# Two cached attention layers and two gated layers on one core: joint sums of a head's two batches, queries of two heads at once, and early key units of pass 2 in one eight-tile product

## The chip, the core and the metric

The kernel runs on one core of a Trainium2 chip. The core has a matrix engine (TensorE, PE in the profile, with PEld for its weight loads), a vector engine (DVE), a scalar engine (ScalarE, ACT), GpSimd (POOL) and SyncE (SP), which here only issues DMAs. Its 16 DMA engines move the data from HBM into the on-chip memory SBUF. The metric is the device time of one execution in microseconds (us). The kernel before has a median of 1315.13 us over three runs (1314.31 to 1316.29).

## What is computed

One token for each of two batches (B = 2, D = 448 features) goes through attention, a gated layer, attention and the gated layer again; both layers use the same weights and the same caches each time. The caches are what is large: 16 heads, 4096 cached positions, 256 features, keys and values, float32, read in full in each of the two attention passes.

```python
def _A_ref(x, k_cache, v_cache, wq, wo):          # x: (2, 1, 448), caches: (2, 16, 4096, 256)
    q = (x @ wq).reshape(B, Sq, H, Dh).transpose(0, 2, 1, 3)
    scores = jnp.einsum("bhqd,bhkd->bhqk", q, k_cache) * (Dh ** -0.5)
    p = _softmax(scores, axis=-1)
    o = jnp.einsum("bhqk,bhkd->bhqd", p, v_cache)
    return o.transpose(0, 2, 1, 3).reshape(B, Sq, H * Dh) @ wo

def _B_ref(x, W_gate, W_up, W_down):
    gate = x @ W_gate                              # (448, 1792)
    gate = gate * (gate > 0)
    return (gate * (x @ W_up)) @ W_down

x = x + _A_ref(_layernorm(x), ...)
x = x + _B_ref(_layernorm(x), ...)
x = x + _A_ref(_layernorm(x), ...)
x = x + _B_ref(_layernorm(x), ...)
```

## The kernel before, in words

**Units.** Attention works through 32 units in a pass, one for each head and batch; the two batches of a head stand next to each other, so units 0 and 1 are one head, units 2 and 3 the next. A unit has 4096 keys and 4096 values of 256 floats. On 128 partitions that is 32 tiles of 256 floats for the keys and as many for the values. Eight tiles make a chunk (2048 floats for each partition, 1.05 MB); a unit's keys are four chunks, numbered c = 0 to 3.

**One unit.** The query is spread over all partitions. DVE multiplies the key tiles by it and sums each product to one score; ACT does a share of the sums (`activation` with `accum_out`). In most of a pass (`score_block`) one product covers all 32 tiles (L468) and one reduction sums 24 or 32 of them (L482). In the first five units of pass 2 (`u < HASTE`) and at the end of it (`CLOSING`), `score` goes chunk by chunk: a product of several tiles (L514), sums of some of them on ACT (L520), and for the rest either a reduction (L524) or, tile by tile, a fused product and sum on DVE (L527). Then `softmax_max` takes the maximum (DVE L536, over the partitions by POOL L538), `softmax_exp` the exponentials (ACT L543, L546) and their sum over the partitions (POOL L552), of which DVE takes a reciprocal for a head's two units (L559). `weigh` multiplies the values by the weights on PE (L580): four pairs of tiles go to four groups of rows of one PSUM bank, two rows in each, and the two batches use two banks. `out_copy` (ACT L593) and `out_add` (DVE L596) add a bank's two halves, `out_turn` (PE L606) sums the rows and turns them into a column, `out_keep` (DVE L619) divides, and `project` (PE L629) multiplies by the head's output weights. A wait on another engine stands in an engine's own queue, in the order of the code: what follows it on that engine waits too.

**Queries.** `query(u + 1)`, in every odd unit, makes the queries of the next head for both batches: five matmuls on PE (L414, L418), a copy on ACT (L426) and two broadcasts on POOL (L430). In the chunked units the order on ACT is: sums of chunks 0 to 2, the copy of the query, sums of chunk 3.

**Memory and loads.** SBUF holds an arena of three blocks of eight slots (a slot is one chunk) and three smaller single slots. `pump` issues the loads of a fixed list, in order and all from SP (L154); the next is issued as soon as slots for it are free, so a load is set off by the release of what lay there before. In mid-pass a load is a whole block, 8.39 MB (four chunks of keys of a unit and four of values of the unit before). Some twenty chunks at the start of pass 2 are kept from pass 1 (`keep`), so pass 2 begins with data on chip, and its loads wait for these chunks to be used up. Its units run in the order of heads 15, 14, 0, 1, ... 13. A load has one of eight semaphores in turn, and an SP instruction also waits for the load that used the same semaphore before.

**The gated layer** (`ffn`) follows each pass. Its weights come in seven loads of 0.92 MB (`w_in`) and four smaller ones (`w_out`). During its matmuls the first units of pass 2 have no query yet.

**What the change touches.** `pump` and `source` (loads), `query_weights`, `query_of` and `query`, the choice of tiles in `score` (L502 to L510), `softmax_exp`, `weigh`, `out_copy` to `out_keep`, and the packing of the weights on the host.

Of the kernel before, what the change touches and what calls it, by code (L numbers as in the profile page):

```python
# [15 lines left out]
P = 128  # L16
# [19 lines left out]
SUMS = 96  # L36
HASTE = 5
# [41 lines left out]
def two_layers(  # L79
# [31 lines left out]
    left_at = {}  # L111

    def source(key, n):
# [16 lines left out]
        if kind == "in":  # L130
            return w_in[c]
        return w_out[:, 14 * P * c : min(14 * P * (c + 1), 14 * D)]

    def pump():
        while pending:
# [19 lines left out]
            for k in range(n):  # L155
# [5 lines left out]
                at_of[key] = at + k  # L161
            if n >= NC:
                blocks.add((kind, name))
# [5 lines left out]
    def get(*key):  # L169
        at = at_of[key]  # L170
        return arena[:, place(at) : place(at + 1)]

    def query_weights(h):
        if h >= GROUPED:
            return get("h", h, 0)[:, : F // 2]
        at = h % 2 * F // 2
        return get("q", h // 2, 0)[:, at : at + F // 2]
# [55 lines left out]
    at_end[("k", n_u - 2)] = twos  # L233
# [14 lines left out]
    pending += of_second + [(key, 1) for key in ffn_loads]  # L248
# [22 lines left out]
    junk = down[:, :DH]  # L271
    y_end_row = extra[SUMS : SUMS + B, :TAIL]
# [9 lines left out]
    lead = little("lead", 2, bufs=1)  # L282
    nc.vector.reduce_sum(lead, ident.rearrange("p (m r) -> p r m", r=32)[:, :2], axis=AX.X)
# [86 lines left out]
    def attention(order, after, q_first=None, begun=None):  # L370
# [10 lines left out]
        def query_of(u, pq):  # L381
            h, b = order[u]
            w = query_weights(h)
            for c in range(FULL):
                nc.tensor.matmul(
                    pq[:, b, :],
                    xT[:, c, b : b + 1].to_broadcast([P, P]),
                    w[:, c * DH : (c + 1) * DH],
                    start=(c == 0),
                    stop=False,  # L390
                )
            for j in range(2):
                nc.tensor.matmul(
                    pq[:, b, j * P : (j + 1) * P],
                    xT[:, FULL + j, b : b + 1].to_broadcast([P, P]),
                    w[:, FULL * DH : FULL * DH + P],
                    start=False,
                    stop=(j == 1),
# [3 lines left out]
        def query(u):  # L402
            h = order[u][0]
            w = query_weights(h)
# [7 lines left out]
            q = pq[:33, 0, :]  # L412
            for c in range(FULL):
                nc.tensor.matmul(  # L414
                    q, xs[:, c, :], w[:, c * DH : (c + 1) * DH], start=(c == 0), stop=False
                )
            for j in range(2):
                nc.tensor.matmul(  # L418
                    q[:, j * P : (j + 1) * P],
                    xs[:, FULL + j, :],  # L420
# [570 lines left out]
```

## Time and profile before

| | before |
|---|---|
| median of three runs | 1315.13 us |
| the profiled execution, its own time | 1315.95 us |
| its span (first to last instruction) | 1314.1 us |
| read from HBM | 560.73 MB, 427 GB/s over the span |
| busy: DVE, PE, POOL, ACT | 82%, 43%, 28%, 16% |
| granted TensorE clock, mean | 0.682 |
| instructions | 9066 |

The profiled execution lies 0.82 us above the median of the runs. In the views below, times are from the start of the span. "idle before" in square brackets is how long the engine stood idle before an instruction, and behind the arrow what ended that. PE does each float32 matmul in two passes, so a group of three matmuls is counted as x6. Pass 1 takes the time to about 662 us, the first gated layer to 688 us, pass 2 to about 1288 us. The units of pass 2 stand in the trace as follows: unit 0 from 688.2 us, unit 1 from 699.6, unit 2 from 710.2, unit 3 from 721.4, unit 4 from 734.7, unit 5 from 746.0, unit 6 from 764.7, unit 7 from 782.1, unit 8 from 800.8, unit 9 from 829.8 us (starts of their first product on DVE).

### The profile page before, as it was taken

What the parts mean: (1) busy time and instruction counts of PE and PEld (TensorE: products, weight loads), DVE (VectorE), ACT (ScalarE), POOL (GpSimd) and SP (SyncE); (2) the same over time, 40 slices, a digit from 0 to 9 for tenths busy, and PEclk for the clock granted to TensorE, in tenths of its full rate; (3) what the DMA queues carried; (4) which work ended last, traced back from release to release, by engine and by line L of the source; (5) the groups of instructions that cost most, each with busy time, mean ns of one, the idle gap of its engine ahead of it and who ended that gap; (6) DMA issues with size and microseconds to landing.
All of it is one profiled execution on the core that took longest, in us unless ns stands there. A gap on an engine that the chain in (4) does not pass through costs nothing.

```text
span 1314.1 us, 9066 instructions
## 1 busy us (share of the span) xinstructions
PE 569.9 (43%) x3280; PEld 192.3 (15%) x3280; DVE 1075.0 (82%) x744; ACT 213.3 (16%) x853; POOL 367.5 (28%) x192
## 2 busy tenths in 40 slices
PE   3143343433434334245495544342443434434358
PEld 2011111110111101112141111110111101111113
DVE  4989989799897998787729987698999889886981
ACT  2100000010000000122416523000000000022261
POOL 0332305325053250321001144142345324130220
PEclk9676666666666666677796666666766757667579
DMA  9999999999999999999999999999999999999997
GB/s 407 443 427 431 434 433 427 437 431 429 437 433 429 437 433 418 445 423 430 420 400 418 433 427 443 429 435 433 427 436 431 433 435 433 431 431 427 428 422 326
DMA packets 20216, 561.32 MB, mean 427 GB/s; under 512 B 2248, under 2 KB 2380, under 8 KB 6860
## 3 DMA queue, kind: packets, MB, share of 16 engines
q1 hardware_dynamic: 20164, 560.74, 99.4%
q8 instruction: 26, 0.43, 0.1%
q14 instruction: 18, 0.15, 0.0%
q10 hardware_dynamic: 8, 0.00, 0.0%
HBM read 560.73 MB, written 0.00 MB: 427 GB/s over the span
## 4 chain that ended last, share of the span: by engine, by line
DMA 60%; DVE 28%; PE 6%; POOL 4%; ACT 2%; issue 1%; SPq 0%; DVEq 0%; POOLq 0%; ACTq 0%
DMA arena<-in_vk_dram 54%; DVE tiny L482 11%; DVE arena L468 11%; POOL tiny L538 4%; DMA arena<-in_w_head_dram 3%; DMA arena<-in_w_in_dram 2%; DVE arena L514 2%; DVE arena L527 1%; PE po L580 1%; DMA arena<-in_w_out_dram 1%; DVE row L596 1%; ACT arena L520 1%; PE pq L414 1%; PE small L606 1%; PE acc L629 1%
## 5 line engine op out<-in xcount | busy, mean ns | idle before, releaser
L468 DVE TENSOR_TENSOR arena<-arena 128x8192 f32<-128x8192 f32 (+2 forms) x52 | 441.7, 8497 | 100.8 <-DMA arena<-in_vk_dram 100.7
L482 DVE TENSOR_REDUCE tiny<-arena 128x32 f32<-128x8192 f32 (+2 forms) x53 | 430.2, 8118 | 0.0
L606 PE MATMUL small<-tiny,row 128*128 128x1 f32 x256 | 61.6, 344 | 656.4 <-DVE row L596 656.4
L580 PE MATMUL po<-arena,tiny 128*2 128x512 f32 x2052 | 307.8, 748 | 40.4 <-ACT tiny L546 17.6
L552 POOL PARTITION_ALL_REDUCE tiny<-tiny x64 | 249.9, 3905 | 61.3 <-ACT tiny L546 61.3
L538 POOL PARTITION_ALL_REDUCE tiny<-tiny x64 | 89.3, 1396 | 551.9 <-DVE tiny L536 551.9
L606 PEld LDWEIGHTS small<-tiny,row 128*128 128x128 f32 x256 | 56.1, 306 | 717.6 <-DVE row L596 717.6
L543 ACT ACTIVATE tiny<-tiny 128x1 f32<-128x1 f32 x64 | 18.8, 294 | 580.2 <-POOL tiny L538 580.2
L430 POOL PARTITION_BROADCAST arena<-arena x58 | 27.6, 546 | 288.8 <-ACT arena L426 288.8
L580 PEld LDWEIGHTS po<-arena,tiny 128*2 128x2 f32 x2052 | 54.0, 97 | 239.8 <-issue 197.1
L414 PE MATMUL pq<-arena,xs 128*33 128x256 f32 x174 | 74.6, 595 | 0.0
L520 ACT ACTIVATE arena<-arena 128x256 f32<-128x256 f32 x154 | 62.0, 404 | 42.2 <-DVE arena L514 42.0
L426 ACT ACTIVATE arena<-pq 33x256 f32<-33x256 f32 x29 | 10.9, 377 | 307.6 <-PE pq L418 307.6
L596 DVE SCALAR_TENSOR_TENSOR row<-po,tiny,row 128x256 f32<-128x256 f32 x64 | 30.7, 479 | 35.2 <-ACT row L593 34.9
L629 PE MATMUL acc<-arena,tiny 128*2 128x448 f32 x128 | 49.5, 868 | 21.3 <-DVE tiny L619 18.6
L474 ACT ACTIVATE arena<-arena 128x256 f32<-128x256 f32 x104 | 41.7, 403 | 78.1 <-DVE arena L468 78.1
L514 DVE TENSOR_TENSOR arena<-arena 128x1024 f32<-128x1024 f32 (+2 forms) x25 | 41.9, 1674 | 4.3 <-PE acc L629 4.3
L414 PEld LDWEIGHTS pq<-arena,xs 128*33 128x33 f32 x174 | 25.1, 161 | 66.4 <-issue 65.2
L593 ACT ACTIVATE row<-po,tiny 128x256 f32<-128x256 f32 x64 | 29.1, 455 | 26.7 <-PE po L580 26.7
L520 ACT ACTIVATION_READ_ACCUMULATOR arena<-arena 128x1 f32 x154 | 28.8, 187 | 0.0
L619 DVE TENSOR_TENSOR tiny<-small,tiny 128x4 f32<-128x4 f32 x32 | 5.2, 161 | 28.6 <-PE small L606 28.6
L546 ACT ACTIVATE tiny<-tiny 128x32 f32<-128x32 f32 x64 | 26.4, 413 | 2.2
(153 smaller groups left out, 369.2 us busy)
## 6 DMA issues: line engine op xcount, KB each, us to landing
arena<-in_vk_dram SPq DMA_DIRECT2D x16, 4096.0 KB, 40.1
arena<-in_vk_dram SPq DMA_DIRECT2D x18, 2048.0 KB, 36.1
arena<-in_w_pair_dram SPq DMA_DIRECT2D x11, 1792.0 KB, 30.7
arena<-in_w_in_dram SPq DMA_DIRECT2D x14, 896.0 KB, 23.2
arena<-in_vk_dram SPq DMA_DIRECT2D x12, 1024.0 KB, 10.4
arena<-in_vk_dram SPq DMA_DIRECT2D x1, 6784.0 KB, 39.4
arena<-in_w_head_dram SPq DMA_DIRECT2D x7, 896.0 KB, 8.7
arena<-in_w_out_dram SPq DMA_DIRECT2D x5, 896.0 KB, 8.5
```

Source lines behind the costliest of these rows:

```text
L414: nc.tensor.matmul(q, xs[:, c, :], w[:, c * DH : (c + 1) * DH], start=(c == 0), stop=False)
L468: nc.vector.tensor_mul(part, part, q_of[u][:, None, :].to_broadcast([P, n, DH]))
L474: nc.scalar.activation(kt[:, t, :], kt[:, t, :], AF.Copy, accum_out=s_of[u][:, t : t + 1])
L482: nc.vector.reduce_sum(found, part, axis=AX.X)
L514: nc.vector.tensor_mul(part[:, :whole, :], kt[:, :whole, :], q_of[u][:, None, :].to_broadcast([P, whole, DH]),)
L520: nc.scalar.activation(part[:, t, :], part[:, t, :], AF.Copy, accum_out=found[:, t : t + 1])
L538: nc.gpsimd.partition_all_reduce(mx_of[u], mx, P, RED.max)
L552: nc.gpsimd.partition_all_reduce(total[:, b : b + 1], rs, P, RED.add)
L580: nc.tensor.matmul(po_of[u][32 * t : 32 * t + 2, (i - 2 * t) * DH : (j - 2 * t) * DH], p_of[u][:, n : n + 2], values[:, i * DH : j * DH], ...
L596: nc.vector.scalar_tensor_tensor(row[:, :DH], po_of.pop(u)[:, DH:], lead[:, 1:2], row[:, :DH], op0=ALU.mult, op1=ALU.add,)
L606: nc.tensor.matmul(pT_of[u - u % 2][:, c, b : b + 1], row[:, c * P : (c + 1) * P], ones, start=True, stop=True,)
L629: nc.tensor.matmul(acc[at : at + B], oT_of[h][:, c, :], wo[:, c * D : (c + 1) * D], start=(n < 3), stop=(n >= n_u - 3),)
```

## The change

**Joint sums.** The exponentials of a unit go to one of two rows of 66 floats (`spaced`), in which every pair of weights is followed by a pair of zeros; GpSimd clears the rows at the start of a pass. A matmul of `weigh` takes four columns of it: (w, w, 0, 0) for a head's first unit and (0, 0, w, w) for its second. So both units of a head add up in four rows of one bank, and `out_copy`, `out_add` and `out_turn` run once for a head, in the iteration after its second unit's weights are applied.

**Queries of two heads.** The query weights of heads 2j and 2j + 1 lie interleaved in one slot. In an even head below 14, `query` computes both heads' queries: matmuls of 512 columns instead of 256, one copy of 33x512, two broadcasts of 512 floats. In the odd head it returns at once.

**Early key units.** In the chunked units at the start of pass 2, from chunk 2 of unit 1 on (14 chunks), the product covers all eight tiles, ACT sums five and one reduction on DVE three. Before, the product covered four tiles, ACT summed these four, and four fused products did the rest.

**Loads.** `w_in` is packed side by side, and the first two of its loads in pass 2 are one load into two slots. The keys of unit 30 in pass 2 come in one load instead of two, and so are scored by `score_block`.

```diff
-            return w_in[c]
+            return w_in[:, c * F : (c + n) * F]
...
+    def query_parts(h):
...
+        w = get("q", h // 2, 0)
+        at = [(2 * c + h % 2) * DH for c in range(FULL)]
+        found = [(c, slice(0, DH), w[:, i : i + DH]) for c, i in enumerate(at)]
+        return found + [(FULL + h % 2, slice(0, DH), w[:, 2 * FULL * DH :])]
...
-    at_end[("k", n_u - 2)] = twos
...
-    pending += of_second + [(key, 1) for key in ffn_loads]
+    pending += of_second + [(("in", "", 0), 2)] + [(key, 1) for key in ffn_loads[2:]]
...
         def query(u):
+            if u in q_of:
+                return
...
+            n = 2 if h < GROUPED and h % 2 == 0 else 1
+            q = pq[:33].rearrange("p b n -> p (b n)")[:, : n * DH]
+            parts = query_parts(h)
+            if n == 2:
+                more = query_parts(h + 1)
+                w = get("q", h // 2, 0)
+                joined = [
+                    (c, slice(0, 2 * DH), w[:, 2 * c * DH : 2 * (c + 1) * DH]) for c in range(FULL)
+                ]
+                c, _, w_c = more[-1]
+                parts = joined + parts[FULL:] + [(c, slice(DH, 2 * DH), w_c)]
...
             nc.scalar.activation(found, q, AF.Copy)
-            for v in (u, u + 1):
-                b = order[v][1]
-                q_of[v] = w[:, 2 * b * DH : (2 * b + 1) * DH]
-                nc.gpsimd.partition_broadcast(q_of[v], found[32 * b : 32 * b + 1], channels=P)
+            for i in range(2):
+                b = order[u + i][1]
+                spread = room[:, at[b] : at[b] + n * DH]
+                nc.gpsimd.partition_broadcast(spread, found[32 * b : 32 * b + 1], channels=P)
+                for k in range(n):
+                    assert order[u + i + 2 * k] == (h + k, b)
+                    q_of[u + i + 2 * k] = spread[:, k * DH : (k + 1) * DH]
...
-                whole = by_act if u < HASTE or last else CT
+                whole = by_act if 2 * u + c // 2 < 3 or last else CT
                 if whole == CT:
                     by_act = CT // 2 + 1
...
-            p_of[u] = s_of.pop(u)
+            p_of[u] = spaced[u % 2]
+            found = p_of[u][:, 2:].rearrange("p (k r) -> p k r", r=4)[:, :, :2]
...
-                po_of[u] = po[u % 2]
+                po_of[u] = po[u // 2 % 2]
...
-                            po_of[u][32 * t : 32 * t + 2, (i - 2 * t) * DH : (j - 2 * t) * DH],
-                            p_of[u][:, n : n + 2],
+                            po_of[u][32 * t : 32 * t + 4, (i - 2 * t) * DH : (j - 2 * t) * DH],
+                            p_of[u][:, at : at + 4],
                             values[:, i * DH : j * DH],
-                            start=(c == 0 and i == 2 * t),
-                            stop=(c == NC - 1),
+                            start=(u % 2 == 0 and c == 0 and i == 2 * t),
+                            stop=(u % 2 == 1 and c == NC - 1),
...
         def out_add(u):
-            nc.vector.scalar_tensor_tensor(
-                row[:, :DH], po_of.pop(u)[:, DH:], lead[:, 1:2], row[:, :DH],
-                op0=ALU.mult, op1=ALU.add,
-            )
+            if u % 2:
+                nc.vector.scalar_tensor_tensor(
+                    row[:, :DH], po_of.pop(u)[:, DH:], fold[:, 1:2], row[:, :DH],
+                    op0=ALU.mult, op1=ALU.add,
+                )
...
         first_query()
+        nc.gpsimd.memset(down[:, DH : DH + 2 * SPACED], 0.0)
```

The built programs show where this lands. DVE's queue in unit 2 of pass 2, from its first product to its maximum (`arena` holds keys and products, `tiny` the scores, `row` the head's sums). Before:

```order
L514 TENSOR_TENSOR arena<-arena 128x1024
L527 SCALAR_TENSOR_TENSOR arena,tiny<-arena 128x256 x4
L596 SCALAR_TENSOR_TENSOR row<-po_98,tiny,row 128x256
L514 TENSOR_TENSOR arena<-arena 128x1024
L527 SCALAR_TENSOR_TENSOR arena,tiny<-arena 128x256 x4
L514 TENSOR_TENSOR arena<-arena 128x1024
L527 SCALAR_TENSOR_TENSOR arena,tiny<-arena 128x256 x4
L559 RECIPROCAL tiny<-tiny 128x2
L514 TENSOR_TENSOR arena<-arena 128x1024
L527 SCALAR_TENSOR_TENSOR arena,tiny<-arena 128x256 x4
L536 TENSOR_REDUCE tiny<-tiny 128x1
```

And in the changed program:

```order
L534 TENSOR_TENSOR arena<-arena 128x2048
L544 TENSOR_REDUCE tiny<-arena 128x3
L534 TENSOR_TENSOR arena<-arena 128x2048
L544 TENSOR_REDUCE tiny<-arena 128x3
L534 TENSOR_TENSOR arena<-arena 128x2048
L544 TENSOR_REDUCE tiny<-arena 128x3
L581 RECIPROCAL tiny<-tiny 128x2
L534 TENSOR_TENSOR arena<-arena 128x2048
L544 TENSOR_REDUCE tiny<-arena 128x3
L556 TENSOR_REDUCE tiny<-tiny 128x1
```

The products are twice as wide, a reduction of three tiles stands for four fused products, and the addition of the bank's halves (L596) is gone from this unit; it stands in units 3, 5, 7 and so on only.

PE's queue from the end of unit 1 to unit 5 of pass 2 (`po_98` and `po_99` are the two banks, `pq` the queries, `acc` the sum of the projections). Before:

```order
L606 MATMUL small<-tiny,row 128x1 x2
L580 MATMUL po_98<-arena,tiny 2x512 x8
L629 MATMUL acc<-arena,tiny 2x448 x2
L414 MATMUL pq<-arena,xs 33x256 x3
L418 MATMUL pq<-arena,xs 33x128 x2
L580 MATMUL po_98<-arena,tiny 2x512 x8
L606 MATMUL small<-tiny,row 128x1 x2
L580 MATMUL po_99<-arena,tiny 2x512 x16
L606 MATMUL small<-tiny,row 128x1 x2
L629 MATMUL acc<-arena,tiny 2x448 x2
L414 MATMUL pq<-arena,xs 33x256 x3
L418 MATMUL pq<-arena,xs 33x128 x2
```

And in the changed program:

```order
L631 MATMUL small<-tiny,row 128x2 x2
L602 MATMUL po_102<-arena,down 4x512 x8
L654 MATMUL acc<-arena,tiny 2x448 x2
L435 MATMUL pq<-arena,xs 33x512 x3
L435 MATMUL pq<-arena,xs 33x256 x2
L602 MATMUL po_102<-arena,down 4x512 x24
L631 MATMUL small<-tiny,row 128x2 x2
L654 MATMUL acc<-arena,tiny 2x448 x2
```

The first query here (in unit 3) has twice the columns, and the second (in unit 5) is gone, as is one of two sums of rows (L606).

ACT's queue from unit 2 to unit 5 of pass 2. Before:

```order
L593 ACTIVATE row<-po_99,tiny 128x256
L520 ACTIVATE arena,tiny<-arena 128x256 x12
L426 ACTIVATE arena<-pq 33x256
L520 ACTIVATE arena,tiny<-arena 128x256 x4
L543 ACTIVATE tiny<-tiny 128x1
L546 ACTIVATE tiny<-tiny 128x32
L593 ACTIVATE row<-po_98,tiny 128x256
L520 ACTIVATE arena,tiny<-arena 128x256 x16
```

And in the changed program:

```order
L616 ACTIVATE row<-po_101,tiny 128x256
L540 ACTIVATE arena,tiny<-arena 128x256 x15
L443 ACTIVATE arena<-pq 33x512
L540 ACTIVATE arena,tiny<-arena 128x256 x5
L563 ACTIVATE tiny<-tiny 128x1
L567 ACTIVATE down,tiny<-tiny 128x16x2
L540 ACTIVATE arena,tiny<-arena 128x256 x20
```

ACT sums five tiles of a chunk instead of four, the copy of the query is as wide again and still stands ahead of the sums of unit 3's last chunk, and the copy of the bank's half is left out of every other unit.

More of the change, by code (lines that the diff above doesn't have):

```diff
@@ L36 @@
 SUMS = 96
+SPACED = 2 * NT + 2
 HASTE = 5
@@ L161, in pump @@
                 at_of[key] = at + k
+                if kind == "in" and k:
+                    lies_at[key] = start + k * F
             if n >= NC:
@@ L271, in two_layers @@
     junk = down[:, :DH]
+    spaced = [down[:, DH + i * SPACED : DH + (i + 1) * SPACED] for i in range(2)]
     y_end_row = extra[SUMS : SUMS + B, :TAIL]
@@ L382, in query_of @@
             h, b = order[u]
-            w = query_weights(h)
-            for c in range(FULL):
+            parts = query_parts(h)
+            for c, cols, w in parts:
                 nc.tensor.matmul(
[L386 to L390, printed above, removed]
-                )
[L392 to L398, printed above, removed]
+                    pq[:, b, cols], xT[:, c, b : b + 1].to_broadcast([P, P]), w,
+                    start=(c == 0), stop=(c == parts[-1][0]),
                 )
@@ L960, in _arrays @@
         "w_pair": np.stack(pair),
-        "w_in": np.stack(full),
+        "w_in": np.concatenate(full, axis=1),
         "w_out": np.concatenate(
```

75 lines of the change are left out of this document (42 added, 33 removed).

## The prediction

> **What bounds the kernel now.** I read the page's DMA queues first, since all caches are read twice, and then the share of the DMA engines in short windows.
>
> ```profile
> q1 hardware_dynamic: 20164, 560.74, 99.4%
> ```
>
> The load queue's packets fill 99.4% of 16 engines' span. So the end is set by loads, and other engines count only where they let this queue run dry. Windows of the span (columns: length, PE, PEld, DVE, ACT, POOL busy, granted clock, DMA share, GB/s) show where it is not full:
>
> ```profile
> 0.00:1.00 1.00, 0.00 (x0) 0.00 (x0) 0.06 (x1) 0.00 (x0) 0.40 (x5) 1.00 0.00 0
> 1.00:2.00 1.00, 0.00 (x0) 0.00 (x0) 0.00 (x0) 0.70 (x1) 0.00 (x0) 1.00 0.41 68
> ...
> 669.00:670.00 1.00, 1.00 (x16) 0.38 (x12) 0.00 (x0) 0.00 (x0) 0.00 (x0) 1.00 0.47 194
> 670.00:671.00 1.00, 1.00 (x13) 0.19 (x8) 0.00 (x0) 0.00 (x0) 0.00 (x0) 1.00 0.86 215
> 729.80:732.60 2.80, 2.80 (x18) 1.19 (x22) 2.42 (x9) 0.23 (x3) 0.00 (x0) 1.00 1.07 456
> 757.80:763.00 5.20, 5.20 (x18) 1.75 (x22) 3.60 (x2) 0.00 (x0) 0.00 (x0) 0.50 1.03 438
> 764.00:767.00 3.00, 2.99 (x28) 0.48 (x20) 2.37 (x2) 0.60 (x4) 2.46 (x3) 1.00 1.04 448
> 1300.00:1310.00 10.00, 8.24 (x120) 3.53 (x118) 1.68 (x7) 0.99 (x4) 0.00 (x0) 1.00 0.71 282
> ```
>
> Outside the start, a dip of under one us at 669 and the tail, there is nothing to win. What can be lost is in the chain of waits: early in pass 2 it runs through DVE, PE, ACT and POOL, not through DMA, because the kept chunks are worked off late and loads wait for their slots. It returns to DMA here:
>
> ```profile
> 818.14 31.02 DMA arena<-in_vk_dram
> ```
>
> The load of a block (8.39 MB) is issued at 818.14 and lands at 849.16. The one before it is issued at 800.60, when unit 7's keys are released:
>
> ```profile
> 800.60 0.33 SPq L154 DMA_DIRECT2D arena<-in_vk_dram  x1
> ```
>
> It lands just ahead of unit 9's product, which waited for it:
>
> ```profile
> 829.84 8.69 DVE L468 TENSOR_TENSOR arena<-arena 128x8192 f32<-128x8192 f32 x1 [11.54 <-DMA arena<-in_vk_dram]
> ```
>
> So it takes 829.8 - 800.6 = 29.2 us. The two landings are 849.16 - 829.8 = 19.3 apart, which is one block's transfer, so 29.2 - 19.3 = 9.9 us of earlier loads lay ahead of it. That is the cover: delay unit 7's release by more, and the queue runs dry. At 818.14 it is 31.0 - 19.3 = 11.7 us. A dry queue starts late too: the first load, issued just before 1 us, moves data from some 1.4 us on (share 0.00, then 0.41), which I take as 1.2 us from issue to data.
>
> **The change part by part, up to unit 7's release.** First the early chunks. In unit 1 two products of the present form follow each other; unit 30, at the end, already has the new form (eight tiles, five on ACT, three reduced):
>
> ```profile
> 704.58 1.22 DVE L514 TENSOR_TENSOR arena<-arena,po 128x1024 f32<-128x1024 f32 x1
> 707.08 1.22 DVE L514 TENSOR_TENSOR arena<-arena,po 128x1024 f32<-128x1024 f32 x1
> 710.06 0.19 DVE L536 TENSOR_REDUCE tiny<-tiny 128x1 f32<-128x32 f32 x1 [0.41 <-ACT arena L520]
> 710.17 1.21 DVE L514 TENSOR_TENSOR arena<-arena 128x1024 f32<-128x1024 f32 x1
> ```
>
> ```profile
> 1250.18 2.29 DVE L514 TENSOR_TENSOR arena<-arena 128x2048 f32<-128x2048 f32 x1
> ...
> 1253.94 0.48 DVE L596 SCALAR_TENSOR_TENSOR row<-po,tiny,row 128x256 f32<-128x256 f32 x1 [0.48 <-ACT row L593]
> 1254.34 2.28 DVE L514 TENSOR_TENSOR arena<-arena 128x2048 f32<-128x2048 f32 x1
> ...
> 1257.53 2.28 DVE L514 TENSOR_TENSOR arena<-arena 128x2048 f32<-128x2048 f32 x1
> ...
> 1265.23 0.18 DVE L536 TENSOR_REDUCE tiny<-tiny 128x1 f32<-128x32 f32 x1 [1.18 <-ACT arena L520]
> 1265.33 2.28 DVE L514 TENSOR_TENSOR arena<-arena 128x2048 f32<-128x2048 f32 x1
> ```
>
> A chunk takes DVE 707.08 - 704.58 = 2.50 us now and 1257.53 - 1254.34 = 3.19 in the new form. At a unit's end the maximum waits for ACT 0.41 us now and 1.18 then, since ACT's five sums start only after a product twice as long. Unit 1 (two chunks): 2 x 0.69 + 0.77 = +2.15.
>
> Joint sums take L596 out of units 2 and 4. Unit 30's 1265.33 - 1250.18 = 15.15 holds 0.48 of waiting and 0.40 of L596, which leaves 14.27. Units 2 to 6 start now at
>
> ```profile
> 721.44 1.22 DVE L514 TENSOR_TENSOR arena<-arena 128x1024 f32<-128x1024 f32 x1
> ...
> 734.69 1.23 DVE L514 TENSOR_TENSOR arena<-arena 128x1024 f32<-128x1024 f32 x1
> ...
> 745.98 2.28 DVE L514 TENSOR_TENSOR arena<-arena 128x2048 f32<-128x2048 f32 x1
> ...
> 764.63 0.19 DVE L536 TENSOR_REDUCE tiny<-tiny 128x1 f32<-128x32 f32 x1 [3.19 <-ACT arena L520]
> 764.73 8.68 DVE L468 TENSOR_TENSOR arena<-arena 128x8192 f32<-128x8192 f32 x1
> 774.89 0.48 DVE L596 SCALAR_TENSOR_TENSOR row<-po,tiny,row 128x256 f32<-128x256 f32 x1 [1.47 <-ACT row L593]
> ```
>
> so units 2 and 4 take 11.27 and 11.29: +3.0 each. In unit 5 the query falls away. ACT's sums of its last chunk stood behind the copy of that query and so behind PE, which is the 3.19 us that DVE waited: -3.2. In unit 6 L596 falls away too, but not all of the 1.47 us before it: the reciprocal behind it still waits for POOL's sum of the exponentials. Between nothing and 1.9 us saved I take 0.3, L596's part after that sum.
>
> Unit 3 has the joint query. DVE reaches its third chunk's end after 3 x 3.19 + 0.48 + 0.40 + 0.2 for the way to PE = 10.65 us. Then PE projects and computes the query, ACT copies it, sums five tiles, and only then comes the maximum. PE's rows now, in unit 3 and in unit 5:
>
> ```profile
> 729.77 0.92 PE L629 MATMUL acc<-arena,tiny 128*2 128x448 f32 x4 [0.56 <-DVE tiny L619]
> 730.62 1.48 PE L414 MATMUL pq<-arena,xs 128*33 128x256 f32 x6
> ...
> 732.47 1.04 PE L580 MATMUL po<-arena,tiny 128*2 128x512 f32 x8
> ```
>
> ```profile
> 757.77 1.66 PE L629 MATMUL acc<-arena,tiny 128*2 128x448 f32 x4 [6.50 <-DVE tiny L619]
> 759.36 2.77 PE L414 MATMUL pq<-arena,xs 128*33 128x256 f32 x6
> ...
> 762.92 1.49 PE L580 MATMUL po<-arena,tiny 128*2 128x512 f32 x8
> ```
>
> At full clock a projection takes 0.85 us and a query 732.47 - 730.62 = 1.85; at half clock (windows 729.8 and 757.8 above) 1.59 and 3.56. A query of twice the columns: 0.85 + 2 x 1.85 = 4.55, or 1.59 + 2 x 3.56 = 8.71. For ACT (L426 takes 0.28 ahead of the sums, say 0.5 at 33x512, and a tile 0.40) and the maximum, 2.75. Unit 3 then takes 17.95 to 22.1 us against 13.25 now: +4.7 to +8.9. Which clock? PE idled 0.56 us before the fast query and 6.50 before the slow one, where full clock came by 764, some 6 us after its work began. In the new order PE waits about 2 us for a longer chunk: I take 3 us of half clock and the rest full, 3.0 / 1.92 = 1.57 of the 4.55 done, 2.98 left, 6.0 in all, so +6.15.
>
> The Trainium skill, TensorE: Matmul & The Clock Gate, Part 1, says that the clock is halved until a window of about 3.4 us has been busy, and halved again after an idle one. By that, 8.7 us of half-clock work cannot stay slow to its end, and the lower price of unit 3 would hold or the middle one (1316.5 or 1317.9), but not +8.9 (1320.7). The row at 757.8, 5.2 us of busy PE at 0.50, agrees only if its first window began part idle.
>
> Delay at unit 7's release (unit 7 itself keeps its L596): 2.15 + 3.0 + 6.15 + 3.0 - 3.2 - 0.3 = **10.8 us**, between 9.35 and 13.55. Against the cover: 10.8 - 9.9 + 1.2 = 2.1 us of dry queue. To this comes something for the 16 engines: that landing is of the last of them. In 1300 to 1310 they are on average idle for 29%, 2.9 us, because they end unevenly, and a pause takes the early ones' lead. Between 0 and 2.9 I take 0.9, nearer to nothing, since the late one may stay the late one. Unit 8's product also waits for two broadcasts of a joint query; its release has 11.7 us and the pause before it as cover.
>
> Costs put at nothing, with the queue that hides them. DMA issues by line, with size and median us to landing, of the windows 709.9 to 710.4, 734.5 to 735 and 1020 to 1140, and of the whole span:
>
> ```profile
> arena<-in_vk_dram SPq DMA_DIRECT2D x1, 2048.0 KB, 11.7
> ```
>
> ```profile
> arena<-in_vk_dram SPq DMA_DIRECT2D x2, 4096.0 KB, 29.3
> ```
>
> ```profile
> arena<-in_vk_dram SPq DMA_DIRECT2D x6, 43.2
> ```
>
> ```profile
> arena<-in_w_in_dram SPq DMA_DIRECT2D x14, 896.0 KB, 23.2
> ```
>
> After unit 1 a load of 2.1 MB (4.8 us of transfer) has 6.9 us ahead of it and is delayed by 2.15. After unit 3 two loads of 4.2 MB (9.7 each) land after 29.3 on average, so 14.8 lie ahead of the first, and it is delayed by 2.15 + 3.0 + 6.15 = 11.3, at half clock 14.05: covered, if barely. In mid-pass a block has 43.2 - 19.3 = 24 us ahead of it, which hides the later queries, PE's weighing and POOL's broadcasts; if it were used up, each late broadcast would hold the next product and so the next load. The closing loads of `w_in` have 23.2 - 2.1 = 21, which hides unit 30's keys coming as one load and one product.
>
> Windows of the first gated layer, with loads of `w_in` and `w_out`, and of mid-pass:
>
> ```profile
> 670.00:680.00 10.00, 9.18 (x67) 3.17 (x59) 1.84 (x6) 0.88 (x3) 0.00 (x0) 1.00 0.99 397
> 900.00:910.00 10.00, 6.96 (x36) 1.86 (x36) 10.00 (x4) 0.00 (x0) 0.00 (x0) 0.64 1.00 433
> ```
>
> The two joined loads save rows of packets: 1.83 MB of `w_in` at 433 GB/s instead of the 397 of 670 to 680 would save 0.4 us, none is the other end, and I take 0.2.
>
> Sum: 2.1 + 0.9 - 0.2 = +2.8 us. The profiled execution took 1315.95 (span 1314.1, 1.85 around it), so 1318.75 in its terms; it lies 0.82 above the median of 1315.13, so the forecast is **1317.9 us**. A measurement of this kernel tells 0.2%, 2.6 us, from no change.
>
> **The rivals.** *The cover holds.* If PE has its full clock at the joint query, the delay is 9.35, the dry time 9.35 - 9.9 + 1.2 = 0.65, and with nothing for uneven engines and -0.2 the time is 1315.6. For it: the clock was 1.00 at this place before. Against: longer chunks keep PE idle longer.
>
> *The joint query at half clock throughout*: 13.55 - 9.9 + 1.2 + 0.9 - 0.2 = +5.55, so 1320.7. The rows of unit 5 speak for it, the full clock by 764 against it.
>
> *A steady loss*: in mid-pass 13 joint queries end in wider broadcasts, for which the next unit's product waits. It decides if DVE then no longer catches up with the loads; at 0.5 us each this is +6.5, so 1321.6. Against it speaks the queue in mid-pass.
>
> *Faster*: the tail. If the 16 engines end evenly, the 2.9 us of 1300 to 1310 go, with 0.2 for the joined loads: 1312.0. It needs the pause in pass 2 to stay away and the shorter rows or fewer instruction loads to even out the engines. I see no row that says so.
>
> **How the numbers follow.** Forecast 0.46 (from +1.3 to +4.5, over half of it above 2.6), cover holds 0.20, half clock throughout 0.16, steady loss 0.08, faster 0.10. Slower by over 0.2%: 0.26 of the forecast, 0.16 and 0.08, 0.50; within 0.2%: 0.20 and 0.20, 0.40; faster 0.10. The likeliest alone spans 1316.4 to 1319.6; the range from 1313.5 to 1321.8 takes in the cover that holds and half clock, and leaves out the fast tail and more than the steady loss.
>
> **What would show it.** Right: between 805 and 820 us a DMA share clearly below one; chunk products in units 2 to 4 about 3.2 us apart; unit 5 some 3 us shorter; PE's joint query in unit 3 with part of its window at 0.50; block loads in mid-pass again with some 40 us to land; the closing chain of loads as before. Wrong: DMA share of one through 820 (the cover held), new dips after 850 (a steady loss), or a total of DMA time that itself has changed.

## The result and the profile after

The changed kernel takes 1321.22 us, the median of five runs (1320.95 to 1323.31), against 1315.13 before: a ratio of 1.0051, interval 1.0040 to 1.0061. It is 6.1 us slower; the forecast was 2.8 slower. The profiled execution took 1320.95 (span 1319.2).

The load queue's line of the page after:

```profile
q1 hardware_dynamic: 19876, 560.74, 99.1%
```

The bytes are the same, and now 0.9% of the span is without loads where it was 0.6%. Where, is seen in windows (columns as in the prediction: length, PE, PEld, DVE, ACT, POOL busy, granted clock, DMA share, GB/s). Of the kernel after:

```profile
713.00:717.00 4.00, 1.16 (x8) 0.26 (x12) 3.96 (x3) 2.01 (x10) 3.04 (x2) 0.50 1.01 338
745.00:749.00 4.00, 0.29 (x4) 0.00 (x0) 2.85 (x3) 1.32 (x7) 2.88 (x2) 0.90 1.01 381
806.00:816.00 10.00, 9.35 (x46) 2.03 (x42) 8.40 (x3) 1.08 (x4) 3.39 (x3) 0.82 0.62 242
```

And the same windows of the kernel before:

```profile
713.00:717.00 4.00, 3.61 (x20) 1.48 (x24) 4.00 (x12) 3.12 (x16) 0.00 (x0) 0.50 1.03 432
745.00:749.00 4.00, 0.00 (x0) 0.00 (x0) 3.57 (x7) 1.31 (x7) 2.32 (x1) 0.73 1.11 473
806.00:816.00 10.00, 4.46 (x28) 1.67 (x32) 8.53 (x4) 4.35 (x20) 4.12 (x2) 0.55 1.10 474
```

The large hole stands where the prediction put it: (474 - 242) GB/s for 10 us are 2.3 MB, 5.4 us at 433 GB/s. Two small ones, 94 and 92 GB/s for 4 us or some 0.9 us each, stand behind the releases of units 1 and 3, where the prediction had written "covered". Counted over the trace's packets (each one's bytes spread evenly over its time), the first 345 MB are read 1.4 us later than before, which is what the two small holes took, the first 348 MB 6.6 us later, and the first 560 MB 6.4 us later: nothing more is lost behind 815 us.

The chain of waits after has the load of unit 7's release as

```profile
811.68 23.16 DMA arena<-in_vk_dram
```

It is issued 811.68 - 800.60 = 11.08 us later than before; 10.8 were forecast. It lands 23.16 us after its issue, although nothing lies ahead of it. DVE's maximum at each early unit's end, and the product of unit 9, show how the delay came about:

```profile
712.33 0.19 DVE L556 TENSOR_REDUCE tiny<-tiny 128x1 f32<-128x32 f32 x1 [1.18 <-ACT arena L540]
726.50 0.19 DVE L556 TENSOR_REDUCE tiny<-tiny 128x1 f32<-128x32 f32 x1 [1.18 <-ACT arena L540]
746.11 0.19 DVE L556 TENSOR_REDUCE tiny<-tiny 128x1 f32<-128x32 f32 x1 [5.65 <-ACT arena L540]
760.31 0.19 DVE L556 TENSOR_REDUCE tiny<-tiny 128x1 f32<-128x32 f32 x1 [1.18 <-ACT arena L540]
775.98 0.19 DVE L556 TENSOR_REDUCE tiny<-tiny 128x1 f32<-128x32 f32 x1
811.65 0.19 DVE L556 TENSOR_REDUCE tiny<-tiny 128x1 f32<-128x32 f32 x1
834.87 8.69 DVE L488 TENSOR_TENSOR arena<-arena 128x8192 f32<-128x8192 f32 x1 [4.00 <-DMA arena<-in_vk_dram]
```

Unit 2 takes 726.50 - 712.33 = 14.17 us (+2.9; forecast +3.0), unit 3 takes 19.61 (+6.4; +6.15), unit 4 14.20 (+2.9; +3.0), unit 5 15.67 (-3.1; -3.2). Unit 9's product starts at 834.87 instead of 829.84. PE's joint query in unit 3, and the clock in two windows:

```profile
737.34 1.06 PE L654 MATMUL acc<-arena,tiny 128*2 128x448 f32 x4 [2.27 <-DVE tiny L644]
738.33 5.13 PE L435 MATMUL pq<-arena,xs 128*33 128x512 f32 x10
```

```profile
738.00:741.00 3.00, 3.00 (x6) 0.66 (x5) 2.43 (x2) 0.36 (x2) 0.00 (x0) 0.50 1.01 431
741.00:743.00 2.00, 2.00 (x7) 0.63 (x6) 0.00 (x0) 0.00 (x0) 0.00 (x0) 0.90 0.98 418
```

PE waited 2.27 us, then worked 0.7 us at full clock, some 3.4 us at half clock (738 to 741, and 0.4 us of the next 2, whose mean is 0.90) and the rest at full clock: 737.34 to 743.4, 6.05 us, where 6.0 was forecast.

So the mechanism and the delay are as predicted, and what the delay costs is not: 6.1 us instead of 2.8. Theory A for the experiments: the loss is the pause alone, and pause and restart cost more than the prediction's terms. Its rivals: part of the loss is something else in the change (joint sums, joint queries, loads), or the early products cost time wherever they stand.

### The profile page after: what moved, and what is told of

Its sections match the earlier page's. It is cut to its first block, busy times and chain, and to the rows that moved or that the text cites. A ratio compares the mean times of both kernels' runs of the same rounds, so it can differ in the third digit from the quotient of the medians.

```text
span 1319.2 us, 8299 instructions
## 1 busy us (share of the span) xinstructions
PE 512.6 (39%) x3016; PEld 152.2 (12%) x3016; DVE 1076.2 (82%) x611; ACT 199.8 (15%) x812; POOL 316.7 (24%) x168
## 4 chain that ended last, share of the span: by engine, by line
DMA 54%; DVE 32%; POOL 7%; PE 3%; issue 2%; ACT 2%; SPq 0%; POOLq 0%; DVEq 0%
DMA arena<-in_vk_dram 50%; DVE tiny L502 16%; DVE arena L488 10%; POOL tiny L574 4%; DVE arena L534 3%; POOL tiny L558 3%; DMA arena<-in_w_in_dram 3%; DMA arena<-in_w_out_dram 1%; DVE tiny L544 1%; PE small L631 1%; ACT arena L540 1%; DVE arena L547 1%; DVE row L620 0%; ACT down L567 0%; PE pq L435 0%
## 5 line engine op out<-in xcount | busy, mean ns | idle before, releaser
L602 PE MATMUL po<-arena,down 128*4 128x512 f32 x2052 | 319.9, 744 | 191.1 <-ACT down L567 122.2
L558 POOL PARTITION_ALL_REDUCE tiny<-tiny x64 | 115.6, 1807 | 702.1 <-DVE tiny L556 701.5
L631 PE MATMUL small<-tiny,row 128*128 128x2 f32 x128 | 31.2, 348 | 562.6 <-DVE row L620 562.6
L574 POOL PARTITION_ALL_REDUCE tiny<-tiny x64 | 178.4, 2787 | 61.3 <-ACT down L567 61.3
L602 PEld LDWEIGHTS po<-arena,down 128*4 128x4 f32 x2052 | 66.3, 98 | 415.4 <-issue 226.5
L631 PEld LDWEIGHTS small<-tiny,row 128*128 128x128 f32 x128 | 28.5, 310 | 594.1 <-DVE row L620 594.1
L435 PE MATMUL pq<-arena,xs 128*33 128x512 f32 (+2 forms) x158 | 73.1, 621 | 0.0
L534 DVE TENSOR_TENSOR arena<-arena 128x2048 f32<-128x2048 f32 (+2 forms) x21 | 45.5, 2168 | 4.5 <-PE acc L654 4.5
L620 DVE SCALAR_TENSOR_TENSOR row<-po,tiny,row 128x256 f32<-128x256 f32 x32 | 15.3, 479 | 24.3 <-ACT row L616 24.3
L567 ACT ACTIVATE down<-tiny 128x32 f32<-128x32 f32 x64 | 26.6, 416 | 2.2
L556 DVE TENSOR_REDUCE tiny<-tiny 128x1 f32<-128x32 f32 x64 | 12.0, 187 | 13.2 <-ACT arena L540 10.0
```

The source lines that it names most:

```text
L435: nc.tensor.matmul(q[:, cols], xs[:, c, :], w_c, start=(i == 0), stop=(i == len(parts) - 1))
L534: nc.vector.tensor_mul(part[:, :whole, :], kt[:, :whole, :], q_of[u][:, None, :].to_broadcast([P, whole, DH]),)
L558: nc.gpsimd.partition_all_reduce(mx_of[u], mx, P, RED.max)
L567: nc.scalar.activation(found, s_of.pop(u).rearrange("p (k r) -> p k r", r=2), AF.Exp, bias=nm, scale=sr[:, b : b + 1], accum_out=rs,)
L574: nc.gpsimd.partition_all_reduce(total[:, b : b + 1], rs, P, RED.add)
L602: nc.tensor.matmul(po_of[u][32 * t : 32 * t + 4, (i - 2 * t) * DH : (j - 2 * t) * DH], p_of[u][:, at : at + 4], values[:, i * DH : j * DH] ...
```

## The experiments

Each time is compared with the kernel before as run beside it (medians 1314.54 to 1314.97).

**The early chunks undone, all else changed.**

```diff
-                whole = by_act if 2 * u + c // 2 < 3 or last else CT
+                whole = by_act if u < HASTE or last else CT
```

> The changed kernel with the early chunks of pass 2 in their old form (four tiles in a product, four fused products). Theory A: the time was lost where the load queue ran dry behind unit 7, since its release came 11.1 us late; a load that is issued into an empty queue needs 23.2 us (811.68 to 834.84 in the trace after) where one of 8.39 MB in a full queue adds 19.3, and the median engine's queue ended 6.6 us behind the release at 800.60, not 9.9. Here the delay at unit 7's release is the joint query in unit 3 (+3 at full clock, +5 at half), less 0.9 for the sums of units 2 and 4, 3.2 for the query of unit 5 and 0.3 in unit 6: between -1.5 and +1. No pause at 800 to 815, median 1314.3 to 1315.8. The 16 engines end unevenly as before (first to last landing of the last load about 5.4 us). Rival B: joint sums and joint queries cost something all through the pass, apart from the pause: then 1316.5 to 1318 with block loads that take longer than before.

Measured: 1314.53 against 1314.88, ratio 0.9997 (0.9988 to 1.0006). Unit 7's release (a line with x3 sums up three issues; it starts with the one that unit 7 releases) and its window:

```profile
799.14 19.26 SPq L156 DMA_DIRECT2D arena<-in_vk_dram  x3
```

```profile
806.00:816.00 10.00, 4.89 (x32) 0.84 (x32) 8.41 (x3) 3.99 (x19) 3.85 (x2) 0.66 1.01 436
```

The release is 1.46 us earlier than before and there is no hole. Joint sums, joint queries and joined loads together cost nothing that this can tell from zero, and win nothing. Rival B falls. One expectation missed: the 16 engines land the last load within 3.4 us here, against 5.4 in the profiled execution before, without any pause. So the tail's unevenness differs between executions and is not the pause's doing.

**The early chunks alone, in the kernel before.**

```diff
-                whole = by_act if u < HASTE or last else CT
+                whole = by_act if 2 * u + c // 2 < 3 or last else CT
```

> The kernel before with only the early chunks in the new form. Delay at unit 7's release: unit 1 2.15, units 2 and 4 4 x 0.69 + 0.77 = 3.53 each (L596 stays), unit 3 the same and up to 1.7 more for a slower single query: 12.7 to 14.4 us. Theory A: 12.7 + 23.2 - 29.2 = +6.7 us in the landing of unit 7's load, up to 8.4; less at the end by nothing; median 1321 to 1323.5, so this part alone is as slow as the whole change or slower. Rival B (the excess over my forecast comes from the joint sums and queries): 12.7 - 9.9 + 1.2 + 0.9 = +4.9 at most, 1320 or less.

Measured: 1322.08 against 1314.88, ratio 1.0058 (1.0045 to 1.0071).

```profile
813.34 18.22 SPq L154 DMA_DIRECT2D arena<-in_vk_dram  x3
```

The release is 12.74 us late and the time is where theory A had it. This part alone makes the whole loss: 12.74 from it and -1.46 from the rest make 11.28, and both together measured 11.08.

**A delay of known length, in the kernel before.** In unit 7 the reductions are followed by redundant ones over tiles summed already (24 and 6 tiles; 24 and 21; 15), which write the same scores again:

```diff
                     nc.vector.reduce_sum(found, part, axis=AX.X)
+                if ahead and u == 7:
+                    for n in [24, 6]:
+                        nc.vector.reduce_sum(found[:, :n], part[:, :n], axis=AX.X)
```

> The kernel before with 30 tiles of unit 7 of pass 2 summed a second time on DVE (24, then 6), ahead of the release of its keys: some 8.2 us of delay at that one place and nothing else changed. Theory A: a load into an empty queue lands 23.2 us after its issue, so 8.2 + 23.2 - 29.2 = +2.2 us, 1317.3; DMA share below one for 2 to 3 us before 810. Rival C (my prediction's terms: cover 9.9, 1.2 to restart, 0.9 for uneven engines): the last engine does not idle, so 0 to +0.4 us, 1315.1 to 1315.5.

> As the run with 30 tiles, with 45 tiles of unit 7 summed twice: some 12.3 us of delay at unit 7's release. Theory A: 12.3 + 23.2 - 29.2 = +6.3 us, 1321.4. Rival C: 12.3 - 9.9 + 1.2 + 0.9 = +4.5 us, 1319.6. Rival B (only part of the changed kernel's loss is the pause): about 2 us in a delay of 11, so 3 here, 1318.

> The kernel before with 15 tiles of unit 7 of pass 2 summed a second time: some 4.1 us of delay at unit 7's release. Theory A (cost = delay less 4.5, not below nothing): 0 to +0.3 us, 1314.9 to 1315.2; unit 7's release at 804.7. Rival D (no cover at all, any delay of a release there costs): +4, 1319.

Measured: 1318.16 (30 tiles; ratio 1.0023, 1.0014 to 1.0032) and 1322.62 (45 tiles; 1.0058, 1.0045 to 1.0070) against 1314.88; 1315.38 (15 tiles; 1.0007, 0.9998 to 1.0016) against 1314.72. DVE in unit 7's maximum, which the release follows, and unit 9's product, which waits for that load; 15 tiles:

```profile
804.61 0.19 DVE L539 TENSOR_REDUCE tiny<-tiny 128x1 f32<-128x32 f32 x1
...
828.70 8.69 DVE L468 TENSOR_TENSOR arena<-arena 128x8192 f32<-128x8192 f32 x1 [6.50 <-DMA arena<-in_vk_dram]
```

30 tiles:

```profile
808.78 0.19 DVE L539 TENSOR_REDUCE tiny<-tiny 128x1 f32<-128x32 f32 x1
...
831.83 8.69 DVE L468 TENSOR_TENSOR arena<-arena 128x8192 f32<-128x8192 f32 x1 [5.46 <-DMA arena<-in_vk_dram]
```

45 tiles:

```profile
813.11 0.19 DVE L539 TENSOR_REDUCE tiny<-tiny 128x1 f32<-128x32 f32 x1
...
836.26 8.69 DVE L468 TENSOR_TENSOR arena<-arena 128x8192 f32<-128x8192 f32 x1 [5.57 <-DMA arena<-in_vk_dram]
```

One delay at one place, nothing else changed, and the time follows: 4.04, 8.20 and 12.53 us late cost 0.7 (not told from nothing by its interval; rival D falls), 3.3 and 7.7. Between the last two the slope is 4.5 / 4.33, one for one, and the cost sets in at a delay of 4.9 us (8.20 - 3.28). The prediction's terms (9.9 - 1.2 - 0.9) had put that point at 7.8, so rival C falls. By the landing of the last engine two readings differ from the prediction. A load issued when the queue is at its end lands 831.83 - 808.80 = 23.0 us after its issue (813.13 to 836.26: 23.1), 1.7 more than the 19.3 + 1.2 + 0.9 = 21.4 of the prediction. And with 15 tiles the load, though issued 4 us later than before, lands at 828.7, not 829.84: in the profiled execution before the last engine came later, and the cover was read off that. Theory A itself had kept the 829.84, and so expected 1.1 to 1.4 us too little in both of the longer runs.

The packets show the same without the last engine. With 15, 30 and 45 tiles the first 347 MB are read 0.0, 3.7 and 8.0 us later than before, and the first 560 MB -0.1, 3.6 and 7.8 us later: all that is lost is lost at this place.

The Trainium skill, DMA: Bandwidth & Descriptors (Anatomy of one DMA), gives a DMA issued by GpSimd a fixed 2.0 us plus its bytes at 436 GB/s, which for this one would be an estimate of 21.2 us. These loads are issued by SP, for which that section has no figure; in the eight runs with such a load its first engine lands after 21.2 to 21.4 us, its last after 21.9 to 23.4. The same page (Why a DMA increments its semaphore by 16 and not by 1) says that up to 16 engines finish independently and only the full count means that the data has landed. That agrees with what the trace has of the load ahead of unit 7's: its first engine ended at 806.6 and its last at 810.5 before, 806.5 and 809.3 with 15 tiles.

**Queries of one head again, all else changed.**

```diff
-            n = 2 if h < GROUPED and h % 2 == 0 else 1
+            n, side = 1, h % 2 * DH
...
-                found, at = room[:33, : n * DH], [2 * DH, 4 * DH]
+                found, at = room[:33, side : side + DH], [2 * DH + side, 4 * DH + side]
```

> The changed kernel with each head's query made by itself again; joint sums, new early chunks and loads stay. Theory A (as the first runs sized it: what the load queue loses is the delay of unit 7's release less 4.5 us): the delay is the 12.7 us measured with the early chunks alone, less 0.5 each in units 2, 4 and 6 where L596 falls away: 11.2, so +6.7, 1321.6; the joint query cost nothing in sum, as unit 5 gave back what unit 3 took. Rival B (joint queries cost time through the pass): 1318.5 or less.

Measured: 1322.47 (1319.88 to 1322.69) against 1314.72, ratio 1.0053 (1.0041 to 1.0065).

```profile
812.48 17.94 SPq L156 DMA_DIRECT2D arena<-in_vk_dram  x3
```

0.9 us above what theory A expected, within the spread of the runs, and rival B falls here too. The release is 0.8 us later than in the changed kernel: what the joint query costs in unit 3 unit 5 gives back, with a little over.

**The joined loads undone.**

```diff
+    at_end[("k", n_u - 2)] = twos
...
-    pending += of_second + [(("in", "", 0), 2)] + [(key, 1) for key in ffn_loads[2:]]
+    pending += of_second + [(key, 1) for key in ffn_loads]
```

> The changed kernel with the pair of w_in loads of pass 2 split again and unit 30's keys in two loads again. My prediction gave the joined loads 0.2 us: 1321.4. If they evened out the 16 engines at the end, first to last landing of the last load goes from 2.9 back to some 5.4 us and the time rises by 1 to 2 us, 1322.3 to 1323.3.

Measured: 1321.24 against 1314.72, ratio 1.0049 (1.0037 to 1.0061); the last load lands within 3.6 us. The joined loads are worth nothing that can be measured, and do not even out the tail.

**TensorE kept busy ahead of the joint query of unit 3**, with unread matmuls (of 512, 512 and 384 columns, then of 512 and 320):

```diff
+            if ahead and u == 3:
+                for n in (8, 8, 6):
+                    busy(n)
             if not closing:
                 if_pair(out_keep, u - 2)
```

> The changed kernel with three unread matmuls (512, 512 and 384 columns) on TensorE in unit 3 of pass 2, in the 2.3 us that it waits ahead of the projection and the joint query. If the granted clock follows how busy the 3.3 us before were, projection and query run at full clock: 4.55 us instead of 6.05, unit 7's release comes 1.5 us earlier (810.2) and the time falls by as much, to 1319.7. If the clock does not follow this: no gain, or 0.3 us later by the matmuls put in, 1321.2 to 1321.5. If the pause does not turn delay into time one for one: less than 0.7 us of gain though the release is earlier.

> The changed kernel with two unread matmuls (512 and 320 columns) on TensorE in unit 3 of pass 2, where three (512, 512, 384) ended 1.4 us too late (738.76 instead of 737.34) and so ate what the query won (3.63 us instead of 5.13). If these end by 737.4: projection and query 4.7 us instead of 6.05, unit 7's release near 810.4 instead of 811.7, and, one for one, 1319.9. If the clock in that place hangs on something else, the query takes 5.1 again and the time stays at 1321.2.

PE with three matmuls:

```profile
735.32 3.53 PE L341 MATMUL pq<-ident 128*2 128x512 f32 x5
738.38 0.54 PE L654 MATMUL acc<-arena,tiny 128*2 128x448 f32 x1
...
739.86 3.63 PE L435 MATMUL pq<-arena,xs 128*33 128x512 f32 x10
```

With two:

```profile
735.38 2.40 PE L341 MATMUL pq<-ident 128*2 128x512 f32 x3
737.52 0.54 PE L654 MATMUL acc<-arena,tiny 128*2 128x448 f32 x1
...
738.73 3.63 PE L435 MATMUL pq<-arena,xs 128*33 128x512 f32 x10
```

The clock, with three and with two (0.50 in this window of the changed kernel):

```profile
738.00:741.00 3.00, 2.94 (x10) 0.63 (x10) 2.55 (x2) 0.48 (x3) 0.00 (x0) 1.00 1.02 437
```

```profile
738.00:741.00 3.00, 3.00 (x11) 0.68 (x7) 2.61 (x2) 0.54 (x4) 0.00 (x0) 1.00 1.01 431
```

The query takes 3.63 us instead of 5.13 in both, so the clock there does follow how busy PE was just before; the Trainium skill, TensorE: Matmul & The Clock Gate (Part 1), has it so, with a window of about 3.4 us. With three matmuls they themselves end 1.4 us late and eat this up: 1320.80 against 1314.72 (1.0058, 1.0035 to 1.0080; one run of twelve at 1339.4 widens it), release at 811.70. With two the release comes at 810.59, 1.1 us earlier than after, and the time is 1320.04 against 1314.54 (1.0042, 1.0029 to 1.0055): about 0.6 us nearer to the kernel beside it, in the right direction, though the intervals overlap and the time alone shows nothing.

**The loads at that place cut.** Unit 9's load of 8.4 MB needs the slots of unit 7's keys, while those of unit 6 lie free for 18 us. Cut into keys and values it fits there. First unit 9's load alone (`range(10, 29)`), then those of units 9, 10 and 11; ACT's share of a unit's sums is kept apart from this constant:

```diff
-WHOLE_SECOND = range(9, 29)
+WHOLE_SECOND = range(12, 29)
...
-            shared = 0 if (WHOLE_SECOND if ahead else WHOLE_FIRST)[0] <= u < ALONE else CT
+            shared = 0 if (9 if ahead else WHOLE_FIRST[0]) <= u < ALONE else CT
```

> The changed kernel with unit 9's load of pass 2 cut into its keys and its values (4.2 MB each), nothing else. Both then fit where unit 6's keys and unit 5's values lay, so they are issued when unit 6 releases its keys (793.1) and no longer when unit 7 does (811.7); all products stay as late as they are. Theory A: no pause at 808 to 813, but unit 10's load, released by unit 8 at 830.7, is as late against the queue (which now ends at 829): the pause moves to 829 to 832, the loss stays near 6 us, 1320 to 1321.5. Rival E (the early products themselves cost the time, at whatever place): the same time without any pause.

> The changed kernel with the loads of units 9, 10 and 11 of pass 2 cut into keys and values. Unit 9's parts are issued at 793, unit 10's at 811.7 (unit 7's release, now with some 18 us of earlier loads ahead of it), unit 11's at 830.7. Theory A: DMA share of one from 750 to 900 though unit 7's release comes 11 us late as before; only the small gaps near 714 and 746 stay: 1314.7 to 1316.5. Rival E (the early products cost the time, not the queue): 1321.

Unit 9 alone: 1320.51 against 1314.54, ratio 1.0044 (1.0031 to 1.0057). Its windows:

```profile
806.00:816.00 10.00, 8.33 (x44) 1.98 (x42) 8.67 (x3) 0.59 (x1) 4.40 (x3) 0.88 1.00 433
826.00:834.00 8.00, 1.54 (x16) 0.20 (x8) 7.90 (x3) 0.00 (x0) 4.05 (x1) 0.89 0.82 313
849.00:853.00 4.00, 1.06 (x12) 0.37 (x16) 2.95 (x3) 0.80 (x3) 1.38 (x2) 0.97 0.75 262
```

The hole at 806 to 816 is gone and stands at 828 to 831, as expected, and in a second piece at 850, which was not foreseen; rival E, which had no hole anywhere, does not fit. Three units: 1318.40 against 1314.54, ratio 1.0029 (1.0016 to 1.0041), 2 us above the expectation. Its windows:

```profile
806.00:816.00 10.00, 9.53 (x46) 2.04 (x42) 8.44 (x3) 1.32 (x5) 3.20 (x3) 0.81 1.04 449
831.00:891.00 60.00, 21.92 (x102) 5.96 (x106) 53.19 (x14) 3.71 (x12) 27.53 (x7) 0.66 1.00 425
890.00:894.00 4.00, 3.44 (x32) 0.64 (x24) 1.43 (x2) 1.32 (x4) 2.18 (x4) 1.00 0.78 262
```

No hole now until unit 10's release at 870.69, where the queue thins out for about a microsecond, and another at 891: counted over the packets the reading is 1.7 us later than before at 345 MB (the two small holes), 1.9 at 370, 3.1 at 380, 4.4 at 400 and 4.0 at 560, and the time is 3.9 us longer. Between 831 and 891 DVE never waits for a load; its idle time is that for ACT, PE and POOL within a unit. From unit 9 on it does all 32 tiles, at 20 us a unit, no faster than loads come. So the arrears are not worked off, only met later. That points to the last run: ACT goes on summing eight tiles through unit 15.

```diff
-            shared = 0 if (9 if ahead else WHOLE_FIRST[0]) <= u < ALONE else CT
+            shared = 0 if (16 if ahead else WHOLE_FIRST[0]) <= u < ALONE else CT
```

> As the run with three units' loads cut, and ScalarE goes on to sum eight tiles of a unit through unit 15 instead of through unit 8, so that DVE reduces 24 tiles instead of 32 there. In the run before, DVE worked from 831 to 891 without a wait at 20.2 us a unit, no faster than loads come, so the 11 us stayed in arrear until unit 10's release at 870.7 emptied the queue at 871 and unit 11's at 891. With 24 tiles a unit takes 2.1 us less on DVE: unit 10's release near 866.5, where some 6 us of loads lie ahead of it, more behind that. Theory F (a delay costs nothing where loads lie ahead of it and DVE then has time to catch up): DMA share of one from 750 to 1290, unit 7's release still at 811 to 812, 1314.6 to 1316.5 by the gaps at 714 and 746. Rival E (the early products cost the time themselves): 1318.4 as before, or above.

Measured: 1315.82 against 1314.97, ratio 1.0009 (1.0000 to 1.0018). SP's issue at unit 7's release, and windows:

```profile
811.68 0.33 SPq L156 DMA_DIRECT2D arena<-in_vk_dram  x1
```

```profile
806.00:816.00 10.00, 9.47 (x46) 2.05 (x42) 8.33 (x3) 1.15 (x5) 3.26 (x3) 0.81 1.00 429
831.00:891.00 60.00, 24.20 (x122) 6.38 (x122) 47.18 (x14) 14.08 (x63) 29.34 (x10) 0.69 1.02 439
890.00:894.00 4.00, 1.29 (x8) 0.30 (x12) 1.30 (x1) 0.00 (x0) 0.00 (x0) 0.72 0.99 426
```

All early products are those of the changed kernel, unit 7's release is as late as there to the hundredth, and the loss is 0.85 us instead of 6.1. Rival E falls. What stays is no more than the holes near 714 and 746, which this kernel still has (340 and 393 GB/s in the two windows shown of the kernel after): the reading is 1.5 us late at 345 MB and still 1.5 at 560. The run changes two things at once, and the kernel before with the same cut loads and the same share of ACT was not run, so what these would win there by themselves is not shown. It does not beat the kernel before, and no run here does.

All runs with unit 7's release late and the load uncut, by delay against 800.60, cost against the kernel before beside it, and how much later than in the trace before the first 347 MB are read, counted over the packets:

| run | delay, us | cost, us | delay - cost | 347 MB later, us | delay - that |
|---|---|---|---|---|---|
| 15 tiles twice | 4.04 | 0.7 | | 0.0 | |
| 30 tiles twice | 8.20 | 3.3 | 4.9 | 3.7 | 4.5 |
| two unread matmuls | 9.99 | 5.5 | 4.5 | 5.4 | 4.6 |
| the change | 11.08 | 6.1 | 5.0 | 6.6 | 4.5 |
| three unread matmuls | 11.10 | 6.1 | 5.0 | 6.5 | 4.6 |
| loads undone | 11.42 | 6.5 | 4.9 | 6.8 | 4.6 |
| query undone | 11.88 | 7.8 | 4.1 | 7.3 | 4.5 |
| 45 tiles twice | 12.53 | 7.7 | 4.8 | 8.0 | 4.5 |
| early chunks alone | 12.74 | 7.2 | 5.5 | 8.2 | 4.5 |

Eight kernels of four kinds lie on one line: the cost is the delay less 4.9 us, within some 0.8, and the interval of a single cost is wider than that (the change: 5.3 to 8.0). The bytes, which do not hang on how the engines end, lie on it to a tenth: what is read late is the delay less 4.5 to 4.6 us.

## Why the prediction was right or wrong

Right: that the kernel gets slower, the place, and the mechanism. Each term of the delay held (sum 10.8 forecast, 11.08 measured), the mixed clock of the joint query among them: 3.4 us at half clock (3 forecast), 6.05 us in all (6.0), and the early chunks alone carry it. Right too that sums, queries and loads are hidden in mid-pass: undoing the early chunks leaves a ratio of 0.9997. The bounds held the time (1313.5 to 1321.8), but for the wrong reason: the forecast's own span ended at 1319.6, and the result lies where the rivals were.

Wrong: the step from delay to time, "10.8 - 9.9 + 1.2 = 2.1 us of dry queue" with 0.9 for uneven engines. Its three terms together let the first 7.8 us of delay go free; the runs show 4.9 in time and 4.5 in bytes.

The term that failed most is the cover of 9.9 us. It was read off the landing of the last of 16 engines, and in an execution in which that came 1.1 us later than in the run with 15 tiles. Most engines run dry earlier. In the seven runs of the table in which all of them stood idle before the load was issued, an average engine had read what lay ahead at 807.0 us, once the reading's own lateness at 345 MB is taken off: 6.4 us behind 800.60. The 0.9 for uneven engines was meant for this gap of 3.5 us, but was put "nearer to nothing, since the late one may stay the late one".

The restart was sized at the first byte, 1.2 us, and this was about right: the packets show the first data 1.0 us after the issue, and an average engine starts after 1.1 to 1.4. But its first packet of 64 KiB then takes 2.9 to 3.2 us on average where later ones take 2.4, so that a restart costs 1.8 to 1.9 us. Put right, 11.08 - 6.4 + 1.9 = 6.6: the bytes are 6.6 us late, and the time is 6.1 longer.

Wrong in the small: the loads behind units 1 and 3, "covered, if barely". These covers too were read off the last engine: the first engine's landings in the trace before leave 4.6 and 11.5 us instead of 6.9 and 14.8, against delays of 2.3 and 11.5. There the engines stood idle for only 0.1 and 0.3 us on average, but the first packets of the new load took up to 1.9 and 2.1 us where others of their size take 0.6 and 1.2. Why this already happens with 2.3 us in hand behind unit 1 is not shown. In the changed kernel these 1.4 us cost nothing more: they put off the end of the queue by as much, and so shorten the pause behind unit 7. In the run with cut loads and no pause they are what is left.

The rivals: the cover did not hold. The joint query at half clock throughout gave almost the measured time (1320.7), yet the windows at 738 and 741 show it did not happen: a near hit is no evidence. A steady loss is excluded by the bytes, 6.6 us late at 348 MB and 6.4 at 560. How evenly the engines end differs between executions: 5.4 us from first to last engine before, 2.9 after, 3.4 and 3.6 in runs without a pause or without the joined loads.

## What to carry to other kernels

Where loads bound a kernel, as here, an engine's lateness is free only up to the queue that lies ahead of the load it releases, less what a restart takes; beyond that it costs one for one, and it stays in arrear until some engine works faster than the loads come. Measure that limit by a run with a known delay rather than by one landing: the last of 16 engines makes the queue look longer (9.9 us) than it is for an average one (6.4). And look where slots lie free while a large load waits for others: cutting the load, with spare capacity behind it, gave back 5 of 6 us without undoing the cause.

## What the runs showed that was not expected

A load of 8.39 MB issued when the queue is at its end landed 23.0 to 23.2 us after its issue in five of these runs (23.4 with the loads undone, 22.85 with two unread matmuls, 21.9 with the query undone), against 19.3 between landings in a full queue. The landing of the same, undelayed data stream differs by about 1.1 us between executions, since one of the 16 engines ends later or less late: the load ahead of unit 7's landed at 810.5 before and at 809.3, 810.3 and 809.5 with 15, 30 and 45 tiles. And cutting three loads did not remove the loss but moved part of it 60 and 80 us on, as DVE ran at the pace of the loads and had nothing to catch up with.
